# Linear attention and a GELU MLP on one core: the first group's blocks, the first weight piece and group 1's first product rearranged

## The chip, the cores and the metric

The kernel is one program on one NeuronCore of a Trainium2 chip. The core has a matrix engine (TensorE, "PE" in the profile, its weight loads shown apart as "PEld"), a vector engine (VectorE, "DVE"), a scalar engine (ScalarE, "ACT"), a general engine (GpSimd, "POOL") and a queue engine (SyncE, "SP"). Each runs its own list of instructions in order and waits on semaphores for the others. Data moves between the main memory and the on-chip memory (SBUF) by DMA transfers that SP and POOL issue; matrix products land in eight PSUM banks. The metric is the device time in microseconds (us); less is better.

## The reference, cut to what matters

```python
# attention, per head h, over 12 blocks of 64 positions (B=4, H=8, S=768, D=64)
intra = (q k^T * Dmask) v          # Dmask[i,j] = lam^(i-j) for i >= j, else 0
inter = (q * lam^(i+1)) @ kv_state
out   = intra + inter
kv_state = lam^block * kv_state + (k * lam^(block-1-j))^T v
# then, with x = out laid out as 3072 tokens x 512
h = x @ w_in                        # 512 -> 2048
g = 0.5 * h * (1 + erf(h / sqrt 2))
y = g @ w_out                       # 2048 -> 512, float32 out
```

## The kernel before, in words

**Tiling.** The kernel takes blocks of 128 positions instead of 64. A chunk is one batch entry's 128 positions with all eight heads; chunk n is position block n // 4 of batch entry n % 4, so there are 24 chunks. Four chunks (all batch entries at one position block) form a group of 512 tokens; groups 0 to 5 go through the MLP one after the other. While the PE runs the MLP of group g, the attention of group g + 1 is slipped between its blocks.

**Attention of one chunk.** k, q and v come in as three loads (`load`, line 65, on POOL's queue). k and q are transposed: for chunks 0 to 7 on the PE (`transposed`, line 161), for the others by DMA transposes on SP's queue (`dma_transposes`, line 178). `scores` or `scores_by_quarters` multiply kT and qT; `masked` (line 202) multiplies by the causal mask on DVE. For group 0, `outputs` (line 222) multiplies by v and ACT copies the sum into x. For later groups `visit` (line 594) does up to three things at one place: the part of `done` chunks from the state (`from_states`), the scores of the `asked` chunks, and the part of the `done` chunks from their values (`from_values`), which DVE then scales into x. `next_state` (line 206) makes the next state: four PE products into the bank "kv_ps", then on DVE an add (`tmp`, line 218) and a multiply (`state`, line 219). `decay_v` scales v, on POOL for all but one chunk.

**MLP.** `mm1` (line 420) is one block of the first product: for `ks` slices of 128 features and a range of token columns, four products per slice into the bank "h_ps", then a GELU on ACT into g (line 430). The tag "mh" has two banks, so a third block can't start before ACT has emptied the first. Group 0's second product is plain (`mm2`, 16 blocks). Groups 1 to 5 use `blocks_by_seven` (line 283): seven block products of half the size on sums of g and of w_out, the sums of g being made on DVE (`g_sum`), the results combined on DVE and ACT.

**What sets the order.** Everything is written out by hand; each engine runs its instructions in program order. Around the blocks of group 0 a table `group0` (line 562) gives what runs before block i; N1 = 21 blocks make up the first product, so e + 8 is the ninth block of the second. For later groups `at(when, run)` puts work at a share of a group's cost; B is one block of 30, so 1 + 11 * B is before the twelfth block of group 1. `begin_at` issues a chunk's DMA transposes and its `decay_v`; `prefetch` issues the next loads.

**Loads.** POOL's issues stand in one list (line 97): "k0" is a load of chunk 0's k, "w1" the two transfers (64 partitions each) of weight slices 2 and 3, "w4-5" slices 8 to 11, "w6-7" slices 12 to 15. Weight slices 0 and 1 come in float32 through SP in two transfers of 64 partitions (`wide_w`, line 75) and ACT casts them (line 518). A queue's transfer waits until the one issued eight before it has landed, since there are eight semaphores per kind of queue. `keep_warm` (line 485) issues products on zeros whose results nobody reads.

Of the kernel before, what the change touches and what calls it, by code (L numbers as in the profile page):

```python
# [8 lines left out]
F32 = mybir.dt.float32  # L9
# [6 lines left out]
def kernel(  # L16
# [56 lines left out]
    w_in_r = moe_w_in.rearrange("(c ko d) f -> c d ko f", c=2, ko=NK1)  # L73
    w_out_r = moe_w_out.rearrange("(ko ki) f -> ki ko f", ki=128)
    wide_w = sum_pool.tile([128, NK1, 256], F32, tag="g1", name="wide_w")
    for c, p in enumerate(HALVES):
        nc.sync.dma_start(wide_w[p], w_in_r[c, :, :, :256])

    pos = consts.tile([128, 1], F32)
    row = consts.tile([128, C], F32)  # L80
# [13 lines left out]
        f = NK2 // NS  # L94
        nc.gpsimd.dma_start(w_out_t[:, s * f:(s + 1) * f, :], w_out_r[:, s * f:(s + 1) * f, :])

    for item in "k0 q0 v0 k1 q1 v1 w1 k2 q2 v2 w2 w3 k3 q3 v3 w4-5 w6-7".split():
        if item[0] == "w":
            load_w_in(2 * int(item[1]), 4 if item[2:] else 2)
        else:  # L100
            load(int(item[1]), item[0])
# [45 lines left out]
    def bank(shape, dtype, tag, name):  # L147
        return ps.tile(shape, dtype, tag=tag, name=name, bufs=2 if tag in ("sc", "mh", "mo") else 1)
# [18 lines left out]
        setattr(c, name + "T", dst)  # L167
        empty(dst, t_ps)

    def transposes(c):  # L170
        if c.early:
            transposed(c, "k", "mo", nc.scalar.copy)
            transposed(c, "q", "mo", nc.vector.tensor_copy)
        else:
            transposed(c, "k", "mh", nc.scalar.copy)
            transposed(c, "q", "mh", nc.vector.tensor_copy)

    def dma_transposes(c):
        c.kT = work_pool.tile([128, HP, C], BF16, tag="kT", name="kT", bufs=4)
# [26 lines left out]
    def next_state(c):  # L206
        if c.sb == NB - 1:
            return
        kv_ps = bank([128, HP, 128], F32, "t", "kv_ps")
        for hp in range(HP):  # L210
            nc.tensor.matmul(kv_ps[:, hp, :], c.k[:, 2 * hp:2 * hp + 2, :], c.v_dec[:, 2 * hp:2 * hp + 2, :],  # L211
                             start=True, stop=True)
        new = work_pool.tile([128, HP, 128], BF16, tag="state_f", name="state", bufs=8)
        if c.sb == 0:
            nc.vector.tensor_mul(new, kv_ps, lam_c_b)
        else:
            tmp = work_pool.tile([128, HP, 128], F32, tag="tmp", name="tmp")
            nc.vector.tensor_add(tmp, kv_ps, states[c.n])  # L218
            nc.vector.tensor_mul(new, tmp, lam_c_b)  # L219
        states[c.n + M] = new  # L220
# [62 lines left out]
    def blocks_by_seven(g, g_t, first):  # L283
# [18 lines left out]
        def with_sums(i, run):  # L302
            def both():
                run()
                if 10 <= i < 15:
                    g_sum((5, 2, 1, 6, 7)[i - 10], 0)
            return both

        done = [cost for _, cost in first]
        blocks = [(with_sums((sum(done[:i]) + 4 * M * C - 1) // (4 * M * C), run), cost)  # L310
                  for i, (run, cost) in enumerate(first)]
# [103 lines left out]
    def mlp_blocks(g):  # L415
        T = M * C
        x_t = xT[g]
        g_t = g_pool.tile([128, NK2, T], BF16, tag="g", name="g_t")

        def mm1(kf, ks=1, cols=slice(0, T)):  # L420
            n = cols.stop - cols.start

            def run():
                h_ps = bank([128, ks, n], F32, "mh", "h_ps")
                for k in range(ks):
                    for ki in range(NK1):
                        nc.tensor.matmul(h_ps[:, k, :], w_in_t[:, ki, (kf + k) * 128:(kf + k + 1) * 128],  # L427
                                         x_t[:, ki, cols], start=(k == 0 and ki == 0), stop=(ki == NK1 - 1),
                                         skip_group_check=True)
                nc.scalar.activation(g_t[:, kf:kf + ks, cols], h_ps, ACT.Gelu)  # L430
            return run

        om = {}

        def mm2(io, part):
            def run():
                if part == 0:
                    om[io] = bank([128, d_model], F32, "mo", "o2_ps")
                for kf in range(part * 4, part * 4 + 4):
                    nc.tensor.matmul(om[io], g_t[:, kf, io * C:(io + 1) * C], w_out_t[:, kf, :],  # L440
                                     start=(kf == 0), stop=(kf == NK2 - 1))
                if part == NK2 // 4 - 1:
                    o_sb = out_pool.tile([128, d_model], F32, tag="o_s", name="o_sb")
                    nc.scalar.copy(o_sb, om[io])
                    nc.sync.dma_start(out_r[g, :, io, :], o_sb)
            return run

        parts = NK2 // 4
        if g > 0:
            paired = [kf for k in range(NK2 // 2) for kf in (k, k + NK2 // 2)]  # L450
            plan = [(kf, 1, slice(0, T)) for kf in paired]
            if g == 1:
                plan = [(kf, 1, slice(0, T // 2)) for kf in paired[:8]]
                plan += [(kf, 1, slice(T // 2, T)) for kf in paired[:8]] + [(kf, 1, slice(0, T)) for kf in paired[8:]]
            return blocks_by_seven(g, g_t, [(mm1(kf, n, cols), 4 * n * (cols.stop - cols.start))
                                            for kf, n, cols in plan])
        two, three, third, fourth = slice(0, 2 * C), slice(0, 3 * C), slice(2 * C, 3 * C), slice(3 * C, T)
        plan = [(kf, 1, two) for kf in range(6)] + [(0, 4, third), (4, 2, third)]
        plan += [(kf, 1, three) for kf in range(6, 12)] + [(kf, 4, fourth) for kf in range(0, 12, 4)]
        plan += [(kf, 1, slice(0, T)) for kf in range(12, NK2)]  # L460
        assert len(plan) == N1
        blocks = [(mm1(kf, n, cols), 4 * n * (cols.stop - cols.start)) for kf, n, cols in plan]
        blocks += [(mm2(io, part), 4 * 512) for pair in range(0, M, 2) for part in range(parts)
                   for io in (pair, pair + 1)]
        return blocks
# [34 lines left out]

    make_powers()
    nc.scalar.activation(warm, pos, ACT.Gelu)
    keep_warm(11, cols=512)
    c = early(0)
    causal(0)
# [9 lines left out]
    keep_warm(3, new=False)  # L515
    transposed(c, "q", "mo", copy)
    outputs(live[0])
    nc.scalar.copy(w_in_t[:, :, :256], wide_w)
    keep_warm(2)
    scores(c)  # L520
    keep_warm(9, new=False)
    outputs(live[1])
    c = early(2)
    transposed(c, "k", "mh", copy)
    transposed(c, "q", "mo", copy)
    keep_warm(1)
    for n in range(3):
        decay_v(live[n], nc.gpsimd)
    for s in range(2):
# [27 lines left out]
    def both_transposed(c):  # L557
        transposed(c, "k", "mh", nc.vector.tensor_copy)
        transposed(c, "q", "mo", nc.vector.tensor_copy)
# [21 lines left out]

    todo = []
# [59 lines left out]
    done = 0  # L642
# [42 lines left out]
```

## Time and profile before

| | |
|---|---|
| median of 3 runs | 209.4 us (209.27 to 211.88) |
| the profiled execution | 209.79 us, of which 208.0 us lie between its first and last instruction (the span) |
| PE busy | 196.2 us (94%) |
| DVE, ACT, POOL busy | 140.9, 80.4, 97.6 us |
| PE, first product of group 0 begins | 16.76 us |
| PE, group 1 begins | 53.43 us; its seven products 70.91 us |
| PE, groups 2, 3, 4, 5 begin | 87.62, 117.50, 148.69, 178.13 us |

The times in the trace count from the span's start. A busy PE means that a matmul is in flight, so 94% leaves little idle time; what the table can't show is which of the few gaps sit on the path to the end, and this is what the views used below are for.

### The profile page before, as it was taken

The numbers are of one execution on the slowest core, as the hardware profiler recorded it, in microseconds if no ns is written. First come the engines' busy times: TensorE is split into PE (matmuls) and PEld (weight loads), VectorE is DVE, ScalarE is ACT, GpSimd is POOL, SyncE is SP. The second block draws the span as 40 slices with busy tenths as digits, with TensorE's granted clock in tenths as the row PEclk, the third lists the DMA queues.
The fourth block names the chain that finished last, engine by engine and source line by source line (L and its number), as shares of the span: only waits on it lengthen the run. The fifth ranks groups of instructions, "written<-read, shape, count | busy, mean of one in ns | idle before, by whom it ended". The sixth has DMA issues, their size and how long they took to land.

```text
span 208.0 us, 4700 instructions
## 1 busy us (share of the span) xinstructions
PE 196.2 (94%) x1975; PEld 131.5 (63%) x1993; DVE 140.9 (68%) x223; ACT 80.4 (39%) x149; POOL 97.6 (47%) x115
## 2 busy tenths in 40 slices
PE   7599899999999997999999997999999999999992
PEld 2367675455775686855488754488755588544882
DVE  4374704946687969888968889939888848123482
ACT  6826466042565520064630162630164520466200
POOL 8989983689947999386750196100100000000000
PEclk9999999999999999999999999999999999999999
DMA  5999999999999999999999399900310000500014
GB/s 90 156 165 175 192 206 196 156 207 134 110 213 159 139 157 143 153 143 248 156 139 129 122 169 119 149 3 3 136 67 3 0 0 3 202 0 3 0 50 151
DMA packets 101412, 24.68 MB, mean 119 GB/s; under 512 B 92944, under 2 KB 98576, under 8 KB 101392
## 3 DMA queue, kind: packets, MB, share of 16 engines
q0 software_dynamic: 79712, 13.37, 91.0%
q1 hardware_dynamic: 21680, 11.02, 28.3%
q8 instruction: 15, 0.25, 0.5%
q14 instruction: 5, 0.04, 0.1%
HBM read 27.27 MB, written 6.29 MB: 161 GB/s over the span
## 4 chain that ended last, share of the span: by engine, by line
PE 79%; DMA 11%; POOL 4%; DVE 2%; issue 1%; ACT 0%; POOLq 0%; ACTq 0%
PE h_ps L427 36%; PE r_ps L323 8%; PE p_ps L323 8%; PE q_ps L323 8%; PE o_ps L440 6%; PE s_ps L323 4%; DMA w_in_t<-in_moe_w_in_dram 4%; DMA qT<-q_t 4%; DMA v_t<-in_v_dram 3%; PE sc_ps L198 3%; PE o_ps L249 2%; PE kv_ps L211 2%; PE o_ps L239 2%; POOL k_t L67 1%; POOL q_t L67 1%; DVE state L219 1%
## 5 line engine op out<-in xcount | busy, mean ns | idle before, releaser
L430 ACT ACTIVATE g_t<-h_ps 128x512 bf16<-128x512 f32 (+2 forms) x109 | 59.5, 546 | 83.5 <-PE h_ps L427 81.4
L427 PE MATMUL h_ps<-x_t,w_in_t 128*128 128x512 bf16 (+3 forms) x474 | 88.8, 332 | 1.8 <-DMA w_in_t<-in_moe_w_in_dram 0.9
L427 PEld LDWEIGHTS <-w_in_t 128*128 128x128 bf16 x488 | 43.4, 98 | 36.3 <-issue 2.8
L159 POOL TENSOR_TENSOR v_dec<-v_t,lam_m 128x512 bf16<-128x512 bf16 x23 | 24.9, 1101 | 42.5 <-PE kv_ps L211 34.5
L297 DVE TENSOR_TENSOR g_sum<-g_t 128x1024 bf16<-128x1024 bf16 x50 | 34.1, 729 | 12.7 <-ACT g_t L430 12.7
L323 PEld LDWEIGHTS <-g_sum 128*128 128x128 bf16 x400 | 38.7, 98 | 4.9
L204 DVE TENSOR_TENSOR sc_m<-sc_ps,cmask 128x512 bf16<-128x512 f32 x40 | 25.3, 681 | 5.2 <-PE sc_ps L198 5.1
L67 POOL DMA_DIRECT2D k_t<-in_k_dram x24 | 21.9, 911 | 3.7 <-DMA w_out_t<-in_moe_w_out_dram 1.7
L67 POOL DMA_DIRECT2D v_t<-in_v_dram x24 | 21.4, 890 | 3.2 <-DMA w_out_t<-in_moe_w_out_dram 1.7
L67 POOL DMA_DIRECT2D q_t<-in_q_dram x24 | 21.5, 894 | 2.6 <-DMA w_out_t<-in_moe_w_out_dram 2.5
L323 PE MATMUL r_ps<-w_sum,g_sum 128*128 128x256 bf16 x160 | 19.1, 273 | 0.0
L323 PEld LDWEIGHTS <-g_t 128*128 128x128 bf16 x160 | 15.7, 98 | 2.9
L257 DVE TENSOR_TENSOR x_t<-o_ps,lam_q 128x512 bf16<-128x512 f32 x20 | 12.8, 683 | 3.9 <-PE o_ps L249 3.9
L219 DVE TENSOR_TENSOR state<-tmp,lam_c 128x512 bf16<-128x512 f32 x16 | 14.8, 928 | 0.5
L440 PE MATMUL o_ps<-w_out_t,g_t 128*128 128x512 bf16 x60 | 14.6, 380 | 0.1
L218 DVE TENSOR_TENSOR tmp<-kv_ps,state 128x512 f32<-128x512 f32 x16 | 11.0, 689 | 4.6 <-PE kv_ps L211 4.5
L490 PE MATMUL idle_ps<-idle 128*128 128x256 bf16 (+1 forms) x33 | 9.8, 445 | 1.2 <-DVE idle L104 1.2
L361 DVE TENSOR_TENSOR o_sb<-f_e,p_ps 128x512 f32<-128x512 f32 x5 | 3.4, 686 | 9.7 <-issue 9.7
L440 PEld LDWEIGHTS <-g_t 128*128 128x128 bf16 x64 | 5.8, 98 | 6.2
L323 PE MATMUL s_ps<-w_sum,g_sum 128*128 128x256 bf16 x80 | 9.6, 273 | 0.0
L323 PE MATMUL p_ps<-w_out_t,g_sum 128*128 128x256 bf16 x80 | 9.6, 273 | 0.0
L323 PE MATMUL p_ps<-w_sum,g_t 128*128 128x256 bf16 x80 | 9.6, 273 | 0.0
(65 smaller groups left out, 161.7 us busy)
## 6 DMA issues: line engine op xcount, KB each, us to landing
out_dram<-o_sb SPq DMA_DIRECT2D x9, 512.0 KB, 2.8
k_t<-in_k_dram POOLq DMA_DIRECT2D x24, 128.0 KB, 7.9
q_t<-in_q_dram POOLq DMA_DIRECT2D x24, 128.0 KB, 7.9
v_t<-in_v_dram POOLq DMA_DIRECT2D x24, 128.0 KB, 8.2
w_out_t<-in_moe_w_out_dram POOLq DMA_DIRECT2D x4, 512.0 KB, 10.5
out_dram<-o_sb SPq DMA_DIRECT2D x5, 256.0 KB, 5.6
w_in_t<-in_moe_w_in_dram POOLq DMA_DIRECT2D x4, 256.0 KB, 8.6
w_in_t<-in_moe_w_in_dram POOLq DMA_DIRECT2D x6, 128.0 KB, 6.0
```

Of the source, the lines that this page charges most:

```text
L67: nc.gpsimd.dma_start(raw[n, name], chunk_of(name, n))
L159: eng.tensor_mul(c.v_dec, c.v, lam_m[:, :, None].to_broadcast((128, H, D)))
L204: nc.vector.tensor_mul(c.sc_m[:, :, hi, :], c.sc_ps[hi], mask)
L218: nc.vector.tensor_add(tmp, kv_ps, states[c.n])
L219: nc.vector.tensor_mul(new, tmp, lam_c_b)
L257: nc.vector.tensor_mul(x, o_ps[hi], lam_q[:, hi:hi + 3:2, None, :].to_broadcast((128, 2, 2, C)))
L297: nc.vector.tensor_tensor(gsum[i][:, ks, :], g_t[:, ka + k:ka + k + n4, ta], g_t[:, kb + k:kb + k + n4, tb], op=op)
L323: nc.tensor.matmul(o, left[i](k, slice(u * C, (u + 1) * C)), right[i](k), start=(begin and k == 0), stop=(k == KH - 1), skip_group_check=True)
L427: nc.tensor.matmul(h_ps[:, k, :], w_in_t[:, ki, (kf + k) * 128:(kf + k + 1) * 128], x_t[:, ki, cols], start=(k == 0 and ki == 0), stop=(ki ...
L430: nc.scalar.activation(g_t[:, kf:kf + ks, cols], h_ps, ACT.Gelu)
L440: nc.tensor.matmul(om[io], g_t[:, kf, io * C:(io + 1) * C], w_out_t[:, kf, :], start=(kf == 0), stop=(kf == NK2 - 1))
L490: nc.tensor.matmul(idle_ps[0][:, :cols], idle[:, :128], idle[:, :cols], start=True, stop=True)
```

## The change

Six things are changed.

- `wide_w` comes in four transfers of 128 partitions instead of two of 64, and its cast by ACT stands before the attention of chunk 0 instead of behind chunk 0's `outputs`.
- In the list of loads the two transfers "w2" come before "v2".
- Group 0's first product begins with slices 0 and 1 for chunk 0 alone, then for chunk 1 alone; then slices 2 to 7 for chunks 0 and 1 together; slices 0 to 7 for chunk 2. Before, slices 0 to 5 were taken for both chunks and slices 0 to 5 for chunk 2. The attention around it is spread otherwise (the table `group0`), with 10 of the idle products taken out and 7 put in.
- The transposes and scores of chunks 6 and 7 move: chunk 7's transposes and the scores of both go from the end of group 0 into group 1.
- Group 1's first product runs in halves of its tokens: 16 blocks on chunks 4 and 5, then 16 on chunks 6 and 7. Before, 8 slices went by halves and 8 whole. The sums of g start behind block 24.
- In groups 2 to 4 the first visit comes one block later; the loads of chunks 12 and 13 are issued before chunk 10's `decay_v`; `next_state` of even chunks uses the bank "o" instead of "t", and those of group 1 come at other places.

```diff
-    for c, p in enumerate(HALVES):
-        nc.sync.dma_start(wide_w[p], w_in_r[c, :, :, :256])
+    for ko in range(NK1):
+        nc.sync.dma_start(wide_w[:, ko, :], w_in_r[:, :, ko, :256])
...
-    for item in "k0 q0 v0 k1 q1 v1 w1 k2 q2 v2 w2 w3 k3 q3 v3 w4-5 w6-7".split():
+    for item in "k0 q0 v0 k1 q1 v1 w1 k2 q2 w2 v2 w3 k3 q3 v3 w4-5 w6-7".split():
...
-        kv_ps = bank([128, HP, 128], F32, "t", "kv_ps")
+        kv_ps = bank([128, HP, 128], F32, "t" if c.n % 2 else "o", "kv_ps")
...
-                plan = [(kf, 1, slice(0, T // 2)) for kf in paired[:8]]
-                plan += [(kf, 1, slice(T // 2, T)) for kf in paired[:8]] + [(kf, 1, slice(0, T)) for kf in paired[8:]]
+                plan = [(kf, 1, half) for half in (slice(0, T // 2), slice(T // 2, T)) for kf in paired]
...
-        plan = [(kf, 1, two) for kf in range(6)] + [(0, 4, third), (4, 2, third)]
-        plan += [(kf, 1, three) for kf in range(6, 12)] + [(kf, 4, fourth) for kf in range(0, 12, 4)]
+        plan = [(0, 2, first), (0, 2, second)] + [(kf, 1, two) for kf in range(2, 8)]
+        plan += [(0, 4, third), (4, 4, third)]
+        plan += [(kf, 1, three) for kf in range(8, 12)] + [(kf, 4, fourth) for kf in range(0, 12, 4)]
...
+    nc.scalar.copy(w_in_t[:, :, :256], wide_w)
     keep_warm(11, cols=512)
...
     group0 = {
-        1: [lambda: scores(live[2])],
-        5: [lambda: outputs(live[2])],
-        6: [lambda: next_state(live[0])],
-        7: [lambda: next_state(live[1])],
-        8: [lambda: both_transposed(live[3])],
-        9: [lambda: next_state(live[2])],
-        10: [lambda: scores(live[3])],
+        0: [lambda: keep_warm(2)],
+        1: [lambda: keep_warm(2), lambda: outputs(live[1]), lambda: k_transposed(live[2]), lambda: keep_warm(3)],
+        2: [lambda: q_transposed(live[2])],
+        4: [lambda: scores(live[2])],
+        6: [lambda: outputs(live[2])],
+        9: [lambda: k_transposed(live[3]), lambda: q_transposed(live[3])],
+        10: [lambda: next_state(live[0]), lambda: scores(live[3]), lambda: next_state(live[1])],
         12: [lambda: outputs(live[3])],
+        13: [lambda: next_state(live[2])],
         17: [lambda: next_state(live[3])],
         e: [w_out_sums, lambda: decay_v(live[4], nc.vector)],
         e + 8: [lambda: transposes(live[4])],
-        e + 9: [lambda: transposes(live[5])],
-        e + 10: [lambda: visit([], [4, 5], "t o")],
-        e + 11: [lambda: transposes(live[6])],
-        e + 13: [lambda: visit([4, 5], [])],
-        e + 14: [lambda: transposes(live[7])],
-        e + 15: [lambda: visit([], [6, 7], "t o")],
+        e + 10: [lambda: transposes(live[5])],
+        e + 11: [lambda: visit([], [4, 5], "t o")],
+        e + 13: [lambda: transposes(live[6])],
+        e + 14: [lambda: visit([4, 5], [])],
     }
...
-        for i, w in enumerate((0.11, 0.14, 0.19, 0.24) if g == 1 else (0.01, 0.12, 0.18, 0.24)):
+        for i, w in enumerate((0.01, 0.035, 0.21, 0.25) if g == 1 else (0.01, 0.12, 0.18, 0.24)):
...
-            for i, w in enumerate((-0.07, 0.0, 0.13)):
+            for i, w in enumerate((-0.07, 0.0)):
                 begin_at(g + w, n + i)
-            at(g + 7 * B, lambda: prefetch(3 * M + 1))
+            at(g + 0.08, lambda: prefetch(3 * M + 1))
+            begin_at(g + 0.13, n + 2)
...
-            visit_at(g + 9 * B, [n, n + 1], [n + 2, n + 3])
+            visit_at(g + 10 * B, [n, n + 1], [n + 2, n + 3])
...
-    at(1 + 2 * B, lambda: visit([2 * M - 2, 2 * M - 1], []))
+    at(1 + 1 * B, lambda: transposes(live[2 * M - 1], "mo"))
+    visit_at(1 + 2 * B, [], [2 * M - 2, 2 * M - 1])
+    visit_at(1 + 5.5 * B, [2 * M - 2, 2 * M - 1], [])
```

More of the change, by code (lines that the diff above doesn't have):

```diff
@@ L168, in transposed, with transposes @@
         empty(dst, t_ps)
[L170 to L176, printed above, removed]
+    def transposes(c, tag="mh"):
+        transposed(c, "k", tag, nc.scalar.copy)
+        transposed(c, "q", tag, nc.vector.tensor_copy)
     def dma_transposes(c):
@@ L304, in both @@
                 run()
-                if 10 <= i < 15:
-                    g_sum((5, 2, 1, 6, 7)[i - 10], 0)
-            return both
-        done = [cost for _, cost in first]
-        blocks = [(with_sums((sum(done[:i]) + 4 * M * C - 1) // (4 * M * C), run), cost)
-                  for i, (run, cost) in enumerate(first)]
+                if i in sums_at:
+                    g_sum((5, 2, 1, 6, 7)[sums_at.index(i)], 0)
+            return both
+        sums_at = list(range(24, 29)) if len(first) > NK2 else list(range(10, 15))
+        blocks = [(with_sums(i, run), cost) for i, (run, cost) in enumerate(first)]
         left = {1: lambda k, t: gsum[1][:, k, t], 2: lambda k, t: gsum[2][:, k, t],
@@ L452, in mlp_blocks @@
             if g == 1:
-                plan = [(kf, 1, slice(0, T // 2)) for kf in paired[:8]]
-                plan += [(kf, 1, slice(T // 2, T)) for kf in paired[:8]] + [(kf, 1, slice(0, T)) for kf in paired[8:]]
+                plan = [(kf, 1, half) for half in (slice(0, T // 2), slice(T // 2, T)) for kf in paired]
             return blocks_by_seven(g, g_t, [(mm1(kf, n, cols), 4 * n * (cols.stop - cols.start))
                                             for kf, n, cols in plan])
-        two, three, third, fourth = slice(0, 2 * C), slice(0, 3 * C), slice(2 * C, 3 * C), slice(3 * C, T)
-        plan = [(kf, 1, two) for kf in range(6)] + [(0, 4, third), (4, 2, third)]
-        plan += [(kf, 1, three) for kf in range(6, 12)] + [(kf, 4, fourth) for kf in range(0, 12, 4)]
+        first, second, third, fourth = (slice(i * C, (i + 1) * C) for i in range(M))
+        two, three = slice(0, 2 * C), slice(0, 3 * C)
+        plan = [(0, 2, first), (0, 2, second)] + [(kf, 1, two) for kf in range(2, 8)]
+        plan += [(0, 4, third), (4, 4, third)]
+        plan += [(kf, 1, three) for kf in range(8, 12)] + [(kf, 4, fourth) for kf in range(0, 12, 4)]
         plan += [(kf, 1, slice(0, T)) for kf in range(12, NK2)]
@@ L517 @@
     outputs(live[0])
-    nc.scalar.copy(w_in_t[:, :, :256], wide_w)
     keep_warm(2)
     scores(c)
[L521 to L526, printed above, removed]
+    early(2)
     for n in range(3):
@@ L555, in place, with k_transposed, q_transposed @@
         return round(f * total) if g == 0 else round(total + (g - 1 + f) * later)
-    def both_transposed(c):
+    def k_transposed(c):
         transposed(c, "k", "mh", nc.vector.tensor_copy)
+    def q_transposed(c):
         transposed(c, "q", "mo", nc.vector.tensor_copy)
```

## The prediction

> **What bounds the kernel now.** I read the page's slices first: PE is busy in nine tenths of every slice after the first two, so the time is the start, plus PE's work, plus its gaps.
>
> ```profile
> PE   7599899999999997999999997999999999999992
> ```
>
> The gaps come from the view of who waited for whom, asked for PE alone (us in total, times, longest), and their places from the chain of work that ended last.
>
> ```profile
> PE t_ps L165 <- DMA k_t<-in_k_dram: 2.0, 1, 2.0
> PE sc_ps L198 <- DMA qT<-q_t: 1.3, 1, 1.3
> PE idle_ps L490 <- DVE idle L104: 1.2, 1, 1.2
> PE h_ps L427 <- DMA w_in_t<-in_moe_w_in_dram: 0.9, 1, 0.9
> PE o_ps L239 <- DVE tmp L218: 0.9, 1, 0.9
> ```
>
> The first and third lie in the prologue. The other three are what this change can touch. The chain (start us, us, what) places two of them:
>
> ```profile
> 17.45 8.37 DMA w_in_t<-in_moe_w_in_dram
> 25.82 0.14 issue
> 25.96 1.46 PE h_ps L427 x8
> ...
> 75.39 7.67 DMA qT<-q_t
> 83.06 0.14 issue
> ```
>
> Twice PE stands still until a transfer lands: at 25.82 us for weight slices 8 to 11 (gate 1), at 83.06 us for chunk 13's qT (gate 2). What PE does earlier ahead of a gate is worth nothing unless the gate moves. The timeline of group 3 shows the last of the three:
>
> ```profile
> 124.27 2.48 DVE L219 TENSOR_TENSOR state<-tmp,lam_c 128x512 bf16<-128x512 f32 x1
> 126.67 0.68 DVE L218 TENSOR_TENSOR tmp<-kv_ps,state 128x512 f32<-128x512 f32 x1
> ...
> 127.41 0.38 PE L239 MATMUL o_ps<-qT,state 64*64 64x128 bf16 x13 [0.91 <-DVE tmp L218]
> ```
>
> The visit takes PSUM bank "t", which DVE frees only when it has added the last "kv_ps"; a state of 2.48 us (median row 0.69) held it up.
>
> **A. The prologue up to gate 1: 0 us.** PE starts the first product at 16.76 now. After the change chunk 0's x is ready at 14.09 (its copy on ACT, 13.51 + 0.58), PE leaves chunk 1's scores at 14.35, and the first block can run at about 14.6: 2.1 us sooner. I follow PE to the block that needs slices 8 to 11. Both plans do 12,288 columns of products ahead of it (6 x 1024 + 24 x 128 + 2 x 1536 before; 2 x 1024 + 6 x 1024 + 32 x 128 after). On the way PE waits for chunk 1's masked scores (DVE until 15.68), chunk 1's x (16.70), chunk 2's masks (its scores now stand two blocks later, so about 20.2), and chunk 3's q, which lands at 22.15 (issued 14.95, 7.2 us to landing). It arrives at about 25.2, before 25.82, and two `next_state` (0.22 each) now fill part of the gap. So the early start ends in a longer wait, if the gate stays. POOL issues the same 21 loads in the same time; only "w2" goes before "v2". The issue of slices 8 to 11 waits for the transfer eight places before it, then "v2" at 16.55, now "w2" at about 16.3, but POOL is busy with chunk 3's v until 16.73 anyway. Bounds: POOL waited 0.22, 0.27 and 0.40 us in this list, so at best 0.9 comes off the gate, of which PE can use 0.7; at worst the four wide transfers hold chunk 0's k (landed 7.99) up, +0.6. The row nearest is the gate itself, unchanged: 0. The cast of `wide_w`, now ahead of chunk 0's copy on ACT, has ACT idle from 9.55 to 13.51 as cover; the two transfers landed at 5.6 and 7.5, four issues of about 0.6 us end 1.2 us later. If they landed after 12.4 the cast (1.05) would delay chunk 0's copy and with it everything.
>
> **B. Gate 1 to group 0's second product: +0.22.** Before, one `next_state` was left behind the gate, now two; a row of four "kv_ps" products takes 0.22.
>
> **C. Group 0's second product: -1.02.** Two times 0.22 for chunk 7's transposes and 0.57 for the scores of chunks 6 and 7 leave it. Nothing new is late: chunk 4's and 5's transposes come no sooner than now, and chunk 5's q landed at 43.1 against a use at about 44.
>
> **D. Group 1's first product: +2.0.** It takes 70.91 - 53.43 = 17.48 now, with 64 products of 0.216 = 13.82, the visits' 0.92 + 0.57 and four "kv_ps" of 0.22: 16.19; so 1.29 are waits. Their kind is in the chain:
>
> ```profile
> 59.55 0.87 PE h_ps L427 x8
> 60.43 0.04 issue
> 60.46 0.60 PE h_ps L427 x4
> 61.06 0.26 PE kv_ps L211 x4
> ```
>
> Two half blocks (4 products of 256 columns) take 0.87, the third 0.60 + 0.04 instead of 0.44: it waits 0.2 us for its bank, since ACT needs 0.38 and the way there and back. A whole block doesn't wait (0.865 on PE, 0.60 on ACT). Work slipped between blocks hides the wait. So a run of n half blocks waits (n-1)/2 times 0.2. After the change the runs are 1, 1, 1, 1, 7, 2, 2, 7, 10: 3 + 3 + 4 waits, 2.0 us; with the 0.3 at its start, where ACT still copies group 0's output, 2.3. The work grows by 0.45 + 0.57 (from C). 16.19 + 1.02 + 2.3 = 19.5, +2.0. Bounds 1.2 to 3.0 of waits. The seven products then start at 70.91 + 0.22 - 1.02 + 2.0 = 72.1. DVE has cover: the masks of chunks 6 and 7 end at about 59.4, their use is at about 59.9.
>
> **E. Gate 2: -0.95.** PE reaches the scores of chunk 13 1.2 us later than now, so of the stall of 1.33 some 0.13 are left; I put 0.4, because the transfers may be a little later. They are issued otherwise: the loads of chunks 12 and 13 stood behind POOL's wait of 3.9 us for chunk 10's v and went out from 64.62; now from about 59.7. But they can't land much earlier: chunk 11's v landed at 68.05 and chunk 12's k at 69.32, one load time behind it, and then six loads and three transposes filled 8 us. Bounds: the whole stall goes (-1.33), or the early loads delay the transposes (rival 1).
>
> **F. Groups 2 to 4: -1.2.** The visit one block later gives DVE 0.865 more, which removes the 0.15 "issue" at the visits of groups 2 and 4 (96.23, 157.14) and most of the 1.0 by which group 3 (31.03) is longer than group 2 (30.04). Bounds -1.45 to 0. The masks and sums on DVE come 0.87 later, and the first of those needed, for the third of the seven products, has about 2 us in group 2 (done by about 105.3, used at 107.29).
>
> **Sum.** 0 + 0.22 - 1.02 + 2.0 - 0.95 - 1.2 = -0.95. Against the profiled execution: 209.79 - 0.95 = 208.84. That execution is 0.39 above the median of the runs shown, so I forecast 208.5 for the median.
>
> **The rivals.** Times on the basis of the median 209.4.
>
> 1. *Early loads delay the transposes (slower).* Chunk 11's qT landed at 74.84, just as its scores began (74.74). Now about three more loads are queued ahead of it; at 0.9 to 1.3 us each it lands 2.7 to 3.9 later, against 1.2 us of new slack, and the stall passes on to gate 2. For it: load latencies of 9 to 11 us there, a full queue. Against it: transposes took 6.3 to 8 us whatever stood beside them. It decides once qT lands after about 76.8. +2.4 on the forecast: 210.9.
> 2. *Gate 1 moves.* `wide_w` lands sooner and the first loads with it, POOL's lane waits go: 0.7 less, and only if gate 2 moves too: 207.6. The granted bytes (235 GB/s at 3 us, 141 to 180 later) speak for a busy start; the latency of 6.3 us, alike for all first loads, against. The Trainium skill, SBUF — State Buffer, "Door 1: The DMA port swizzle", says that 64 partitions reach only 8 of 16 ports and 128 reach all; this would bring `wide_w` sooner, and its summary's "one DMA, not several" would bring it later. By the rows both land before 9.55, so the sum is the same by either.
> 3. *The pile-up on DVE moves rather than goes.* The 2.48 us row coincides with POOL's issues and `decay_v`; shifted by a few us it may hit another visit. F is then 0: 209.7. The change doesn't do there what it seems to.
> 4. *Masks of chunks 6 and 7 are late* by more than the 0.5 us left: 209.1.
> 5. *PE falls back to its slow pace.* Three idle products took 0.85 at 11.62 us, nine took 1.16 at 14.28, though the granted clock reads 1.00; ten idle products go, seven come. If PE ran the stretch up to gate 1 at half pace, some 8 us of products would pass it by 3: 211.5. The Trainium skill, TensorE: Matmul & The Clock Gate, "What's actually happening", has PE slow down after an idle window of about 3.4 us; the longest gap I find here is below 1 us, so it gets little.
>
> **How the numbers follow.** Forecast 48%, rival 1 20%, rival 3 14%, rival 2 10%, rival 4 5%, rival 5 3%. The range 206.8 to 211.2 takes in the forecast with the bounds of D and F, rivals 1 to 4, and leaves out rival 5 and sums of several bounds. A measurement of this kernel tells about 2% (4.2 us) from no change; below 205.2 would need gates 1 and 2 both gone (3%), above 213.6 rivals 1 and 5 together or a stall not seen (5%); within 92%.
>
> **What would show it.** Right: PE's first "h_ps" at about 14.6 and its wait for w_in_t longer than 0.9, ending near 25.9; group 1's first product about 19.5 long, with many short "issue" pieces; little or no wait for qT; no wait for `tmp` in group 3. Wrong: gate 1 well before 25, a wait for qT above 1 us, or new waits of PE for DVE.

## The result, and the profile after

The changed kernel takes 221.08 us (median, 220.69 to 221.74) beside 210.64 us for the kernel before on the same chip (209.27 to 213.23). The ratio is 1.052, 95% interval 1.043 to 1.062: slower by 5%. The forecast was 208.5, the range 206.8 to 211.2. It was wrong, and on the side to which it gave 5%.

Executions of one kernel differ by a microsecond or two here (the kernel before: 208 to 214 in all its executions); so verdicts go by the ratios, which leave disturbed executions out, and times taken from single profiles hold to about 1 us.

The profiled execution took 220.69 us, its span is 218.6 (208.0 before). First the page's slices, PE's busy tenths and its granted clock:

```profile
PE   7241999999899999989999999999999999999993
PEclk9955599999999999999999999999999999999999
```

The loss is in slices 2 to 4, from 5.5 to 22 us. Before, PE was busy there in five to nine tenths; now it is in one to four. The clock reads half in slices 3 to 5; before, it read nine tenths or more throughout. That earlier row doesn't show all: there, too, the four products of a transpose took 0.61 to 0.63 us until 12.3 us and about 0.40 from 16 us on, which are the two paces that they have inside and outside the half clock here. From slice 5 on the row of PE looks as before, only 10 us later. The view of who waited for whom (us in total, times, longest) says for what PE stood still:

```profile
PE t_ps L165 <- DMA k_t<-in_k_dram: 8.6, 2, 4.4
PE t_ps L165 <- DMA q_t<-in_q_dram: 2.9, 1, 2.9
PE idle_ps L486 <- DVE idle L104: 1.2, 1, 1.2
```

The three gates that the forecast argued about, w_in_t, qT and tmp, are gone from this list. In their place stand the first loads of all, k and q of chunks 0 and 1: 11.5 us instead of 2.0. PE's timeline gives the places (start, duration, and in brackets the idle time ahead):

```profile
10.23 0.61 PE L165 MATMUL t_ps<-ident,k_t 128*128 128x128 bf16 x4 [4.17 <-DMA k_t<-in_k_dram]
14.43 0.61 PE L165 MATMUL t_ps<-ident,q_t 128*128 128x128 bf16 x4 [2.94 <-DMA q_t<-in_q_dram]
...
21.11 0.61 PE L165 MATMUL t_ps<-ident,k_t 128*128 128x128 bf16 x4 [4.41 <-DMA k_t<-in_k_dram]
...
24.77 1.06 PE L422 MATMUL h_ps<-x_t,w_in_t 128*128 128x128 bf16 x8
```

Chunk 0's k landed at 10.19 us (before 7.99), its q at 14.33 (8.74), its v at 18.62 (9.73), chunk 1's k at 21.08 (10.59). The first block starts at 24.77; the forecast had it at about 14.6. What held the loads shows in the view of the tile `wide_w` (duration in ns as least/median/greatest, and what ACT waited for) and in the DMA view cut to 16 to 20 us, where the first two rows are the stretch in 40 slices and the others the packets, MB and share of 16 engines by queue (q0 is POOL's queue with all the loads, q1 is SP's with `wide_w`):

```profile
L77 SPq DMA_DIRECT2D wide_w<-in_moe_w_in_dram x4: 518/904/4374, 1.2 to 3.7; - x4
L499 ACT CAST w_in_t<-wide_w x1: 1045/1045/1045, 20.6 to 20.6; 128x1024 bf16<-128x1024 f32 x1
...
  DMA wide_w<-in_moe_w_in_dram: 11.1, 1
```

```profile
DMA  1124998999999999832121111111111111111111
GB/s 35 35 40 55 87 88 76 91 104 152 165 175 173 155 118 91 87 33 45 24 45 33 35 33 35 35 35 35 35 35 35 35 35 35 35 35 35 35 35 35
...
q1 hardware_dynamic: 120, 0.12, 11.0%
```

In the second half of this stretch the 16 engines are busy in one tenth and move 35 GB/s, while PE, ACT and POOL wait. The queue of `wide_w` takes 11.0% of 16 engines: on average 1.8 of its packets are in flight. (Such a share adds up packet times and doesn't count engines; POOL's queue reads 200% in these 4 us of the kernel before.) Its 120 packets in 4 us take 0.110 x 16 x 4 us / 120 = 58.7 ns each. Two engines with one packet each need 512 x 58.7 ns / 2 = 15 us for all of `wide_w`; ACT got it at 20.6.

The trace also keeps every packet's queue, size, start and duration. Counted from these, the 512 packets of `wide_w` run from 2.8 to 20.2 us, mostly two at a time (12.6 us) and hardly ever more (0.4 us). Each of the four transfers ends with two packets of 4 bytes, the last pair at 20.1 and 20.2 us; in the kernel before each of the two transfers ends with 16 of them.

The loads issued meanwhile land one by one, and POOL, whose next issue waits for the load eight places before it, stands still for 2.40, 3.29, 3.39 and 1.78 us, so that everything behind is issued late as well. That the loads wait for their share on those same two engines fits this, but no view names the engine of a packet.

### The profile page after: what moved, and what is told of

The parts are those of the page before. It is cut to its first block, busy times and chain, and to the rows that moved or that the text cites. A ratio compares the mean times of both kernels' runs of the same rounds, so it can differ in the third digit from the quotient of the medians.

```text
span 218.6 us, 4822 instructions
## 1 busy us (share of the span) xinstructions
PE 199.9 (91%) x2038; PEld 135.4 (62%) x2038; DVE 139.1 (64%) x223; ACT 81.8 (37%) x157; POOL 98.0 (45%) x115
## 3 DMA queue, kind: packets, MB, share of 16 engines
HBM read 27.27 MB, written 6.29 MB: 154 GB/s over the span
## 4 chain that ended last, share of the span: by engine, by line
PE 82%; DMA 8%; DVE 5%; POOL 1%; issue 1%; ACT 1%; POOLq 0%
PE h_ps L422 38%; DMA k_t<-in_k_dram 8%; PE r_ps L318 7%; PE q_ps L318 7%; PE p_ps L318 7%; PE o_ps L435 6%; PE s_ps L318 4%; PE o_ps L245 3%; PE sc_ps L194 2%; PE kv_ps L207 2%; PE t_ps L165 2%; PE o_ps L235 1%; DVE sc_m L200 1%; DVE state L215 1%; PE idle_ps L486 1%; PE o_ps L224 1%
## 5 line engine op out<-in xcount | busy, mean ns | idle before, releaser
L422 PE MATMUL h_ps<-x_t,w_in_t 128*128 128x512 bf16 (+3 forms) x536 | 91.8, 320 | 0.6 <-ACT g_t L425 0.2
L425 ACT ACTIVATE g_t<-h_ps 128x512 bf16<-128x512 f32 (+2 forms) x117 | 60.9, 520 | 83.2 <-PE h_ps L422 82.3
L422 PEld LDWEIGHTS <-w_in_t 128*128 128x128 bf16 x536 | 47.5, 98 | 33.7 <-issue 2.9
L159 POOL TENSOR_TENSOR v_dec<-v_t,lam_m 128x512 bf16<-128x512 bf16 x23 | 25.2, 1112 | 39.7 <-PE kv_ps L207 35.4
L293 DVE TENSOR_TENSOR g_sum<-g_t 128x1024 bf16<-128x1024 bf16 x50 | 33.0, 712 | 10.7 <-ACT g_t L425 10.7
L165 PE MATMUL t_ps<-ident,k_t 128*128 128x128 bf16 x32 | 3.7, 252 | 8.6 <-DMA k_t<-in_k_dram 8.6
L168 DVE COPY kT<-t_ps 128x512 bf16<-128x512 bf16 x4 | 1.7, 424 | 13.3 <-PE t_ps L165 13.3
## 6 DMA issues: line engine op xcount, KB each, us to landing
q_t<-in_q_dram POOLq DMA_DIRECT2D x24, 128.0 KB, 10.4
```

The source lines that it names most:

```text
L159: eng.tensor_mul(c.v_dec, c.v, lam_m[:, :, None].to_broadcast((128, H, D)))
L293: nc.vector.tensor_tensor(gsum[i][:, ks, :], g_t[:, ka + k:ka + k + n4, ta], g_t[:, kb + k:kb + k + n4, tb], op=op)
```

## The experiments

**Theory A**: the source of each of the four transfers has the dimensions 2 x 64 x 256, and a transfer is spread only over as many engines as its outer dimension allows, here two; everything else of the loss follows. **Theory B**: another part of the prologue costs it (the early cast on ACT, the idle products taken out and the half clock after it, the order of the loads). **Theory C**: four transfers, or transfers to 128 partitions, are slow in themselves. A second question is whether the forecast's steps B to F hold once this loss is out of the way.

**1. The four transfers undone.**

```diff
-    for ko in range(NK1):
-        nc.sync.dma_start(wide_w[:, ko, :], w_in_r[:, :, ko, :256])
+    for c, p in enumerate(HALVES):
+        nc.sync.dma_start(wide_w[p], w_in_r[c, :, :, :256])
```

> The changed kernel with one part undone: wide_w comes in two transfers of 64 partitions again; the early cast, the new order and everything else stay. Theory A (the four transfers are the whole loss: the outer dimension of their source is 2, only about two of the 16 DMA engines carry them, and every load beside them waits for those two): chunk 0's k lands near 8 us again, PE's first h_ps starts at 14.6 to 16 us, the granted clock stays at 1.00 from 6 us on, and the time is 207.5 to 210, which is the recorded forecast of 208.5 with its terms. Theory B (the early cast on ACT, the removed idle products or the new order of loads cost most of the 11 us): 215 to 221, with PE waiting for k_t or q_t by over 3 us still.

Measured: 211.17 us, ratio 0.9985 (0.995 to 1.002). That is above the 207.5 to 210 expected, but so was the kernel before beside it, with 211.73. The whole loss is gone, with five and a half of the change's six parts still in. First h_ps 13.69. The waits of PE:

```profile
PE t_ps L165 <- DMA k_t<-in_k_dram: 2.0, 1, 2.0
PE h_ps L422 <- DMA w_in_t<-in_moe_w_in_dram: 1.6, 1, 1.6
PE idle_ps L486 <- DVE idle L104: 1.2, 1, 1.2
PE t_ps L165 <- ACT kT L168: 0.7, 1, 0.7
PE o_ps L224 <- DVE sc_m L200: 0.4, 2, 0.2
PE sc_ps L194 <- DMA qT<-q_t: 0.4, 1, 0.4
```

This is the list that the forecast described: a longer wait for w_in_t, a wait for qT of 0.4, none for tmp. One line over 0.5 us was not in it, 0.7 for ACT's copy of a kT. The clock was not as expected either: it fell to 0.50 from about 10 to 13 us.

**2. The four transfers alone**, in the kernel before, with the cast at its old place: the diff of experiment 1 the other way round.

> The kernel before with one part of the change alone: wide_w in four transfers of 128 partitions, its cast at the old place. Theory A (two engines carry them): the loads of chunks 0 to 3 land some 10 us later as in the changed kernel, first h_ps at 24 to 28 us, time 218 to 223. Theory B (the loss is in the early cast, the idle products or the load order): within 2 us of the kernel before.

Measured: 221.34 us, ratio 1.046 (1.035 to 1.058). PE's waits begin as in the changed kernel, with the same totals to the tenth:

```profile
PE t_ps L165 <- DMA k_t<-in_k_dram: 8.6, 2, 4.6
PE t_ps L165 <- DMA q_t<-in_q_dram: 2.9, 1, 2.9
PE sc_ps L198 <- DMA qT<-q_t: 2.9, 1, 2.9
```

Here the cast runs at 23.8 us and all the old idle products stand: neither the early cast nor the missing products is needed for the loss. Theory B falls as its cause.

**3 and 4. The outer dimension 4 and 16.** Bytes, packets, number of transfers and partitions stay. Neither kernel keeps the order of the rows that the other weights have, so they compute another product and serve for the timing alone.

```diff
+    w_in_c = moe_w_in.rearrange("(c ko d) f -> c d ko f", c=4, ko=NK1)      # 16 in experiment 4
     for ko in range(NK1):
-        nc.sync.dma_start(wide_w[:, ko, :], w_in_r[:, :, ko, :256])
+        nc.sync.dma_start(wide_w[:, ko, :], w_in_c[:, :, ko, :256])
```

> The changed kernel, with the rows of the first weight piece taken as 4 x 32 instead of 2 x 64: still four transfers of 128 partitions, as many bytes and packets, but the outer dimension of the source is 4. (The rows come in another order than the rest of the weights have, so the first 256 features are computed on a wrong permutation; the work is the same.) Theory A: four engines carry 512 packets of 1024 bytes, 128 each; at the 58.6 ns that a packet took they need 7.5 us instead of 15, so the loads come some 7 us earlier than in the changed kernel: chunk 0's v near 12, first h_ps at 16 to 19 us, time 209 to 214. Theory C (four transfers, or transfers to 128 partitions, are slow whatever their outer dimension): 220 to 222, first h_ps near 24.8.

> As the run before, with the rows taken as 16 x 8: the outer dimension of the source is 16 (again another order of rows, the same work, four transfers of 128 partitions). Theory A: all 16 engines carry the transfers, wide_w has landed by about 9 us, ACT does not wait for it beyond that, first h_ps at 14.6 to 16 us, time 207.5 to 210, like the run with two transfers. Theory C: 220 to 222.

| outer dimension | time, us | ratio to before | cast of wide_w starts | chunk 0's k, q landed | first h_ps |
|---|---|---|---|---|---|
| 2 (the change) | 221.08 | 1.052 (1.043 to 1.062) | 20.6, ACT waited 11.1 | 10.19, 14.33 | 24.77 |
| 4 | 214.25 | 1.013 (1.004 to 1.021) | 12.9, ACT waited 3.3 | 6.59, 13.24 | 18.52 |
| 16 | 209.79 | 0.993 (0.988 to 0.998) | 9.7, no wait | 6.29, 7.54 | 12.43 |

The time follows the outer dimension. (With 4 it lies 0.25 us above the range expected, with 16 the first h_ps came 2 us sooner than expected.) Theory C falls: four transfers to 128 partitions are as good as any when the dimension is 16. The order of the rows changes along with the dimension here; experiment 5 has the right rows again. The shares of SP's queue from 4 to 8 us, with 4 and then with 16, in the DMA view of each:

```profile
q1 hardware_dynamic: 205, 0.20, 16.9%
```

```profile
q1 hardware_dynamic: 431, 0.39, 32.5%
```

16.9% is 2.7 packets in flight on average, 32.5% is 5.2. The packets themselves say more. With 4 three or four are in flight at once for 6.1 of the 9.1 us in which `wide_w` comes in, and seldom more (0.8 us); with 16 up to 17 are. And each transfer ends with 4 packets of 4 bytes, then with 16, where the change has 2: "two" and "four" are counted there, though no packet names its engine.

**5. Eight transfers of 64 partitions**, with the right rows, an outer dimension of 64.

```diff
     for ko in range(NK1):
-        nc.sync.dma_start(wide_w[:, ko, :], w_in_r[:, :, ko, :256])
+        for c, p in enumerate(HALVES):
+            nc.sync.dma_start(wide_w[p, ko, :], w_in_r[c, :, ko, :256])
```

> The changed kernel with the first weight piece in eight transfers of 64 partitions, one for each half of the rows and each of the four row blocks; the rows are the right ones, the outer dimension of every source is 64. Theory A (the outer dimension decides how many engines carry it): no loss; 209 to 211.5, first h_ps at 12.4 to 14 us, chunk 0's k landed by 8.1. Open between two sizes: with the rows as 16 x 8 the loads landed up to 1.8 us earlier than with two transfers of 64 partitions, and gate 1 came at 24.99 instead of 26.05. If that came from the smaller transfers, this run shows it too (gate 1 near 25.0, about 209.8); if it came from 128 partitions, gate 1 stays near 26 (about 211). Theory C (more transfers as such cost): slower than 214.

Measured: 210.28 us, ratio 0.9988 (0.9948 to 1.0029). No loss from more transfers. Chunk 0's k landed at 6.29, as with 16 x 8 and 1.8 us before the two transfers of 64 partitions; since these are 64 partitions too, it is the division into smaller transfers and not 128 partitions that lets the loads in sooner. `wide_w` itself comes late this way: ACT waited 2.2 us for it and cast it at 11.7, where with 16 x 8 it waited for nothing. Gate 1's weights landed at 24.15. That this is a gain can't be said: the four transfers of slices 8 to 15 took 6.8 us (median) here and 8.9 in experiment 1, but in the four later profiles with the same eight transfers they took 7.4, 8.8, 8.9 and 7.3. And PE's wait only moved on: 1.8 us for chunk 13's qT.

**6. Step F alone**: one line in the kernel before.

```diff
-            visit_at(g + 9 * B, [n, n + 1], [n + 2, n + 3])
+            visit_at(g + 10 * B, [n, n + 1], [n + 2, n + 3])
```

> The kernel before with one line of the change alone: in groups 2 to 4 the first visit comes before the eleventh block instead of the tenth. Forecast's step F: group 3 (117.50 to 148.53 before, 31.03) gets up to 1.0 us shorter, groups 2 and 4 by 0.15 each; after the run with two transfers I expect 30.17 for group 3 and no gain in the others, so 0.85 in all: ratio about 0.996. Rival: it was the other bank for next_state that removed the wait for tmp; then group 3 stays at 31.0 and the time is that of the kernel before.

Measured: ratio 0.9959 (0.9911 to 1.0007). The time alone can't tell it from nothing, the trace can: group 3 takes 30.16 us (117.09 to 147.25) instead of 31.03, groups 2 and 4 are unchanged, and no wait for tmp is left. The state of 2.48 us is still there, at 123.86; PE comes later. The rival, the other bank, is not needed for it.

**7. Idle products in the long waits of the changed kernel.**

```diff
-    keep_warm(11, cols=512)
+    keep_warm(28, cols=512)
...
-    keep_warm(3, new=False)
+    keep_warm(15, new=False, cols=512)
...
-    keep_warm(2, new=False)
+    keep_warm(20, new=False, cols=512)
```

> The changed kernel with idle products in the three long waits of its start: 28 instead of 11 of 512 columns before chunk 0's k, 15 of 512 instead of 3 of 256 before its q, 20 of 512 instead of 2 of 256 before chunk 1's k. Nothing else differs. It prices the half clock of 8 to 27 us. Theory A (the late loads are the loss, the clock a small addition): chunk 1's q still lands near 22, the granted clock reads 0.9 or more from 8 us on, first h_ps at 23.3 to 24.3 instead of 24.77, time 219 to 220.5. Rival 5 of the forecast (the slow pace itself costs about 3 us): 217 to 218.5.

Measured: 221.76 us, ratio 1.055 (1.045 to 1.066); no gain at all. Clock and waits of PE:

```profile
PEclk9999999999999999999999999999999999999999
```

```profile
PE sc_ps L194 <- DMA qT<-q_t: 2.0, 2, 1.2
PE t_ps L165 <- DMA k_t<-in_k_dram: 1.4, 1, 1.4
PE h_ps L422 <- DMA w_in_t<-in_moe_w_in_dram: 1.2, 2, 0.8
```

The first h_ps came at 23.34, 1.43 us sooner, as Theory A had it. But then PE waited 1.2 us for weights and 2.0 for qT, where the changed kernel waits for neither. The half clock of 17 us cost nothing that these times show: the whole DMA timeline is 10 us late, and both gates with it. I had expected 219 to 220.5, and so had not carried my own rule through, that time won ahead of a gate is worth nothing.

**8. Steps C and D undone** in the kernel of experiment 1.

```diff
-                plan = [(kf, 1, half) for half in (slice(0, T // 2), slice(T // 2, T)) for kf in paired]
+                plan = [(kf, 1, slice(0, T // 2)) for kf in paired[:8]]
+                plan += [(kf, 1, slice(T // 2, T)) for kf in paired[:8]] + [(kf, 1, slice(0, T)) for kf in paired[8:]]
...
-        e + 13: [lambda: transposes(live[6])],
-        e + 14: [lambda: visit([4, 5], [])],
+        e + 13: [lambda: visit([4, 5], [])],
+        e + 14: [lambda: transposes(live[7])],
+        e + 15: [lambda: visit([], [6, 7], "t o")],
...
-    at(1 + 1 * B, lambda: transposes(live[2 * M - 1], "mo"))
-    visit_at(1 + 2 * B, [], [2 * M - 2, 2 * M - 1])
-    visit_at(1 + 5.5 * B, [2 * M - 2, 2 * M - 1], [])
+    at(1 + 2 * B, lambda: visit([2 * M - 2, 2 * M - 1], []))
```

> The run with two transfers (the changed kernel without its four), and in it also steps C and D undone: chunk 7's transposes and the scores of chunks 6 and 7 back in group 0, group 1's first product by halves for 8 slices and whole for 8, its next_state places and sums of g as before. Step D measured +2.17 there and step C -0.3. If gate 2 (chunk 13's qT) does not bound: group 1's seven products start about 1.8 us earlier (near 71.3) and the time falls by 1.8, to about 209.3. If gate 2 bounds, as in the kernel before: the wait for qT at chunk 13's scores grows from 0.43 to 1.3 or more, and only 0.5 to 1.0 us of the 1.8 is kept: about 210.3.

Measured: 210.57 us, ratio 1.002 (0.996 to 1.009). Group 1's seven products start at 71.14 instead of 73.15, but group 2 at 88.63 instead of 89.38: of 2.0 us, 0.75 are kept. The chain of work that ended last (start, us, what) shows where the rest stays:

```profile
75.58 8.49 DMA qT<-q_t
84.08 0.14 issue
84.21 0.42 PE sc_ps L194 x16
```

Gate 2 bounds. PE's work ahead of it can't shorten this kernel any further unless chunk 13's qT lands sooner.

**9 and 10. Both parts together, then later loads.** Experiment 9 takes the eight transfers and the undone steps C and D together; experiment 10 also issues the loads of chunks 14 and 15 behind `decay_v` of chunks 12 and 13.

```diff
-            at(g + 11 * B, lambda: prefetch(4 * M - 1))
...
             begin_at(g + 0.57 + 0.03 * i, c_n)
+            if g == 1:
+                at(g + 0.571 + 0.03 * i, lambda c_n=c_n: prefetch(c_n + 2))
```

> The eight transfers of 64 partitions, together with steps C and D undone; the rest of the change stays. Each was run alone and both reached a wait for chunk 13's qT of 1.8 us, its landing near 84 us (83.06 in the kernel before). If gate 2 is set by the DMA traffic and not by what PE does ahead of it: qT lands near 83.5 to 84 again though PE comes some 3 us sooner than in the run with two transfers, the wait grows to about 2.8 us, and the time is 209.5 to 210.5, equal to either part alone within 0.5. If gate 2 moves with the earlier start: 207.5 to 208.5.

> The run before this one, and in it the loads of chunks 14 and 15 issued after chunk 12's and chunk 13's decay_v, some 4 us later, so that six loads (768 KB) no longer stand ahead of the transposes of chunks 12 and 13. This tests the mechanism of the forecast's rival 1, loads that delay transposes, from the other side. If it holds: chunk 13's qT lands 1.5 to 3 us sooner (81 to 82.5), its wait falls to about 1, and the time falls to 207.5 to 209, faster than both kernels. If the transposes take their 8 us whatever stands beside them (what the forecast held against rival 1): qT lands within 0.5 us of the other run, the time is the same, or some 1 to 2 us longer if chunk 14's or 15's transposes are now late for group 2.

Experiment 9: 210.25 us, ratio 0.997 (0.993 to 1.001), as expected no better than either part. But qT landed at 82.34, sooner than I had written, and the wait was 1.2, not 2.8. Experiment 10: 209.64 us, ratio 0.989 (0.984 to 0.995). The last two issues of each DMA view, cut to the transposes of chunks 12 and 13 (67 to 75 us in experiment 9, 71 to 76 in experiment 10; the last column is the median us from issue to landing):

```profile
kT<-k_t SPq DMA_TRANSPOSE x2, 7.7
qT<-q_t SPq DMA_TRANSPOSE x2, 7.8
```

```profile
kT<-k_t SPq DMA_TRANSPOSE x2, 5.2
qT<-q_t SPq DMA_TRANSPOSE x2, 6.1
```

Fewer loads beside them, and the transposes take about 2 us less; in experiment 11, with the same late loads, the two rows read 6.0 and 6.9. So rival 1's mechanism exists, and what the forecast held against it ("transposes took 6.3 to 8 us whatever stood beside them") doesn't hold.

The gate, however, came no sooner in experiment 10. PE itself came 2 us later (its clock had fallen to half from 11 to 18 us), the transposes were issued 1.5 to 3.3 us later, and chunk 13's qT landed at 82.7, no sooner than in experiment 9. I had expected 81 to 82.5, and a time of 207.5 to 209. That PE no longer waits for qT in this profile is thus due to its own delay as much as to the shorter transposes. By the times alone experiments 9 and 10 are not told apart: their intervals overlap.

**11. More idle products in the short waits of experiment 10**, beside that kernel once more on the same chip.

```diff
-    keep_warm(11, cols=512)
+    keep_warm(17, cols=512)
...
-    keep_warm(3, new=False)
+    keep_warm(7, new=False)
...
-    keep_warm(2)
+    keep_warm(3)
...
-    keep_warm(2, new=False)
+    keep_warm(9, new=False)
...
-    keep_warm(3, new=False)
+    keep_warm(10, new=False)
```

> The run with the late loads of chunks 14 and 15, and in it 26 more idle products in the short waits of the start: 17 instead of 11 of 512 columns before chunk 0's k, 7 instead of 3 of 256 before its q, 3 instead of 2 before its scores, 9 instead of 2 before chunk 1's k, 10 instead of 3 before its q. In that run's profile the granted clock fell to 0.50 from about 11 to 18 us after waits of 0.8, 0.65 and 1.2 us, and the first h_ps came at 14.24 us; in the run with the loads early the clock stayed at 1.00 and it came at 12.99. If these waits bring the half clock on: no slice below 0.9 any more, first h_ps near 13.0, and the time falls by up to 1.2 us, to 208.4 to 209.3 beside 209.64. If it comes whatever PE does there, or if gate 1 (its weights land near 24.3) absorbs it: the same time within 0.4.

> The run with the late loads of chunks 14 and 15 once more, on the same chip as the run with more idle products, as its yardstick: 209.0 to 210.0.

Measured: 208.30 us (six executions, 208.18 to 209.44), ratio 0.988 (0.981 to 0.994), beside 209.21 us (208.32 to 210.89) and 0.992 (0.987 to 0.996) for the yardstick. The clock rows, the yardstick first:

```profile
PEclk9969999999999999999999999999999999999999
```

```profile
PEclk9999999999999999999999999999999999999999
```

All six executions have a mean clock of 0.997 or more; of the yardstick's twelve, ten lie between 0.984 and 0.992. So the products keep the half clock out. The first h_ps comes at 13.52 instead of 14.66. PE reaches the seven products at 70.69 (70.25 in experiment 9), and there is no wait for qT, which lands at 81.53, 0.8 sooner than there. How much of the 0.9 us is the clock is not settled, since gate 1's weights landed at 24.29 in its profile and at 26.57 in the yardstick's. This kernel has the lowest median of all that were run, and by its ratio it is 0.6 to 1.9% faster than the kernel before; the intervals of the two ratios overlap, so by them it is not told apart from the yardstick.

## Why the prediction was wrong, step by step

**The step that failed is A**, in its bound: "at worst the four wide transfers hold chunk 0's k up, +0.6", from "four issues of about 0.6 us end 1.2 us later". I priced the transfers by their issues and took their spread over the engines as given. Measured, one issue alone took 4.37 us, `wide_w` was there at 20.6 us and not before 9.55, chunk 0's k landed 2.2 us later and not at worst 0.6, the first h_ps came 10 us later than forecast, and the end moved by 10.4 us in the medians. So the term that the sum put at 0 was worth some 10 us. Undone, the loss was gone (experiment 1); put into the kernel before, it was there (2); it follows the outer dimension (3, 4).

Half of the price was at hand, in the DMA view of the kernel before, cut to 4 to 8 us:

```profile
q1 hardware_dynamic: 307, 0.29, 36.2%
```

SP's queue moved 307 packets with 36.2% of 16 engines, 75 ns for each. Over two engines 512 packets take 256 x 75 ns = 19 us (17.5 in the changed kernel), not a few. That two would carry them, no row of the trace of before shows.

The Trainium skill does state it: DMA: Bandwidth & Descriptors, "Why a DMA increments its semaphore by 16 and not by 1", says that a transfer is spread over the largest number of engines, up to 16, that divides the outermost dimension above 1 on both sides; here that is 2, then 4 and 16 in experiments 3 and 4. The runs agree: 2, 4 and 16 packets of 4 bytes at the end of each transfer, and casts at 20.6, 12.9 and 9.7 us.

**The rest of A.** With two transfers the first h_ps came at 13.69 (forecast 14.6), PE reached gate 1 at 24.50 (25.2) and waited 1.55 until 26.05 (about 25.9). Right: the early start ends in a longer wait.

The other steps are read between the profiles of the kernel before and of experiment 1:

| step | forecast, us | measured, us | from |
|---|---|---|---|
| A + B + C, group 1 begins | -0.80 | +0.07 | 53.43, 53.50 |
| D, group 1's first product | +2.0 | +2.17 | 17.48, 19.65 |
| E, seven products of group 1 | -0.95 | -0.48 | 16.71, 16.23 |
| F, groups 2 to 4 | -1.2 | -0.86 | 31.03, 30.17 in group 3; groups 2 and 4 unchanged |
| sum | -0.95 | +0.90 | spans 208.0, 208.9 |

- *C* said "nothing new is late". A new wait of 0.67 us for ACT's copy of chunk 5's kT is, with the gate's 0.09, most of the difference. But it stands unchanged in experiment 8, where C is undone, so C's moves didn't bring it; which other part did stays open.
- *D*, the bank waits of the half blocks, was right in kind and size. Experiment 8 shows that only 0.75 of it counts, because gate 2 stands behind it.
- *E*: the stall for qT was 0.43, forecast 0.4. But a DVE result (f_x) came 0.23 late right behind it, and some 0.2 more are spread.
- *F*: the wait for tmp went, 0.86 in group 3; the two pieces of 0.15 did not come. It was shown alone in experiment 6. By the timeline group 2 took 29.88 us, not 30.04: the starts 148.69 and 178.13 in the table of before are the chain's, where the timeline has 148.53 and 177.96.

The opening reading, "nine tenths of every slice after the first two", passes over one 8 and two 7s in its own row; no term is worked out from it.

By these two profiles the sum is out by 1.85 us. By the measured ratio, 0.9985 (0.995 to 1.002), everything but the four transfers is not told from no change; the forecast for it, -0.95 of 209.79 or 0.9955, lies at the edge of that interval.

**The rivals.** *1, early loads*: the price was not paid (qT stall 0.43), the mechanism is real (experiments 10 and 11). *2, gate 1 moves*: not shown; its weights land up to 2.7 us apart in profiles of kernels with the same start (23.85 in experiment 9, 26.57 in the yardstick). Its 207.6 takes all of the 0.9 off the forecast; with the 0.7 that PE can use it is 207.8. The rule of the Trainium skill named there (SBUF — State Buffer, "Door 1: The DMA port swizzle"), by which 64 partitions reach only half the ports, is not tested alone: the last transfer of `wide_w` took 5.7 us with 64 partitions and 256 KB (experiment 1), 5.0 with 128 partitions and 128 KB (experiment 4). *3, the pile-up moves*: no wait for tmp in any later group. *4, masks of chunks 6 and 7 late*: no such wait. *5, slow pace*: it did set in, in the changed kernel behind late loads and, for 3.4 us, in experiment 1 without them; experiment 7 took it away without a gain. "The longest gap I find here is below 1 us" left out the wait of 2.0 us in the forecast's own first list. The price of 3 us "if PE ran the stretch up to gate 1 at half pace" was not put to the test, since no run had half clock for all of that stretch without late loads: the first h_ps came 1.1 us sooner in experiment 11 than in the yardstick (3.4 us at half clock) and 1.4 sooner in experiment 7 than in the changed kernel (17.1 us).

The five rivals and six steps have one gap in common: none asked how the source of a transfer is laid out, only when it is issued, what queues before it and how many partitions it fills.

## What to carry to other kernels

Before costing a DMA by its bytes, read the outermost dimension of its source and destination: here 2 instead of 16 made 512 KB land at 20.6 us instead of before 9.7, and held up every other load. Where a kernel stands at DMA gates, look for the next gate before counting a gain: the early start, the clock in experiment 7 and most of what undoing D gave were won and then lost at w_in_t or qT. What shortened the transposes at such a gate was to take other loads out of their way.

## What was unexpected of the hardware

- One transfer can hold up all others: from about 18 to 20 us 35 GB/s were moved in all, with eight loads waiting, against 157 to 195 in the stretches of 4 us from 8 to 28 us of the kernel before.
- The half clock begins after short waits, too. In experiment 10 waits of 0.8, 0.65 and 1.2 us within 5 us were followed by 6.8 us at 0.50 (0.81 in 10 to 12 us, 0.50 until 18); in experiment 9 somewhat shorter waits (0.6, 0.7 and 0.9) were not. The Trainium skill, TensorE: Matmul & The Clock Gate, "What's actually happening", has a free-running window of about 3.4 us, so that the same start may or may not lose it; 6.8 us here, 3.4 in experiment 1 and 17.1 in the changed kernel are near two, one and five such windows.
- A DMA transpose took 7.7 to 7.8 us beside six more loads and 5.2 to 6.9 without them (medians of pairs, experiments 9 to 11).
